# A long convolution and a spectral mix on one core: the places of the positions are permuted so that result weights and stores are neighbours

## The chip, the cores and the metric

The kernel runs on one core of one Trainium2 chip. The core has five engines with instruction streams of their own: TensorE (PE, matrix products; its weight loads are listed as PEld), VectorE (DVE), ScalarE (ACT), GpSimd (POOL) and SyncE (SP, which here only issues transfers). They meet at semaphores. Sixteen DMA engines move data between the chip's main memory (DRAM) and the on-chip SBUF; PE writes to PSUM, eight banks of 512 float32 columns on each of 128 partitions. The metric is the device time of one execution in microseconds (us).

## The reference: what is computed

Two layers, one behind the other. `x` is 8 sequences of 5696 positions with 128 channels, `h` a filter of the same length.

```python
# 1. causal long convolution along the sequence, by FFT of twice the length
Xf = np.fft.rfft(x, n=2*S, axis=1);  Hf = np.fft.rfft(h, n=2*S, axis=0)
v = np.fft.irfft(Xf * Hf[None], n=2*S, axis=1)[:, :S, :]
# 2. spectral mix: the lowest 64 modes are multiplied by complex 128x128 matrices
V = np.fft.rfft(v, axis=1);  Y = np.zeros_like(V)
Yr = einsum("bmd,mde->bme", Vr, w_r) - einsum("bmd,mde->bme", Vi, w_i)
Yi = einsum("bmd,mde->bme", Vr, w_i) + einsum("bmd,mde->bme", Vi, w_r)
Y[:, :64] = Yr + 1j * Yi
u = v + np.fft.irfft(Y, n=S, axis=1)
out = u + np.maximum(u @ w_ch, 0.0)          # (8, 5696, 128) float32
```

## The kernel before

The sequence's 5696 positions are written as 64 q + p, with q from 0 to 88 and p from 0 to 63. The transform is split into a step over q and one over p, both matrix products with constant tables. The 8 sequences go in 4 pairs. For each pair the kernel transforms, multiplies with the filter's transform (`products`) and transforms back over p, which gives Z: 180 rows (90 frequencies over q, real and imaginary) for each p and channel. Z is written to a scratch tensor in DRAM (`zscr`) and read again in the last stage. On the way the 64 lowest modes are summed up from Z (table G). This takes the first 264 us or so; then the modes are multiplied with `w_r`, `w_i` (`mix`), and the last stage begins.

**The last stage** (lines 777 to 932) runs over the four pairs `g_`. For a pair, Z is loaded in 4 chunks of 16 values of p (`load_zt`), into 5 chunk buffers, so 5 chunks ahead; the next load into a buffer is issued behind the u tiles that use it up. From it come two kinds of tile:

- A **u tile** (`u_tile`, `u_z`, `u_c`): 8 values of p, all 89 q, one sequence. 16 matmuls (8 values of p, real and imaginary rows) with Z as weights and 89 columns of table S4, and two with the mixed modes C as weights and 356 columns of table IB, add up in two PSUM banks. One instruction evacuates the 712 columns to float16 into UT, a buffer of 128 channels x 5696 positions, one for each sequence of the pair, with two sets of buffers in turn. It is done by ScalarE in five tiles of eight and by VectorE in three, in the last pair by ScalarE alone.
- A **result tile** (`o_tile`): up to 128 positions x 4. Four matmuls take 128 columns of UT as weights (line 889) and the 256 columns of WI (`w_ch` beside the identity), so that u and u @ w_ch of 128 positions stand in PSUM with the position on the partition. ScalarE takes the relu into R (line 896), VectorE adds u (line 897) into an output buffer, and SP stores it (line 908).

Both kinds take the next of four pairs of PSUM banks (`LSLOT`), so a tile can begin only when the tile four before it has left its banks.

How positions stand in UT: in the order of time, 64 q + p. A u tile of 8 values of p therefore writes groups of 8 float16 values, 64 apart. A result matmul's partition m takes position 44 m + 4 r4 + j, because then one partition's results are neighbours in DRAM: the weights are every 44th column of UT. Two such tiles (`wide`) fill one output buffer and one store of 512 KB, 4 KB a partition; 44 x 128 = 5632 positions leave 64 at the end (`TAIL`), which both sequences of a pair share in one tile of two matmuls. There are 7 wide output buffers and 4 small ones. As the weights span all of UT, a result tile needs all 8 u tiles of its sequence.

The order is written out by hand (lines 910 to 931). A list `todo` holds the result tiles that can be done. Behind each u tile one or two are taken from it (1 + half); in the last pair, where the sequences go one after the other, two, and two or three in the second sequence. A pair's result tiles are put in the list when the pair is done, those of the last pair's first sequence as soon as it is done. What is in the list after the last u tile is done then: the last pair's tail tile and the 11 tiles of the last sequence.

The symmetric tables S4 and IB are loaded for 33 of 64 values of p; `reflect` makes the others by reading backwards. All transfers named here are issued by SP, in the order of the program, so that a store that waits for its add holds up the loads behind it. Each store takes one of 12 semaphores in turn.

Of the kernel before, what the change touches and what calls it, by code (L numbers as in the profile page):

```python
# [4 lines left out]
P = 128  # L5
# [118 lines left out]
def bass_long_conv_fft__then__afno_spectral_mix_kernel(nc, x, h, moe_w_r, moe_w_i, moe_w_ch, out):  # L124
# [3 lines left out]
    J = 64  # L128
# [22 lines left out]
    c, s = np.cos(th), np.sin(th)  # L151
    w1 = np.block([[c, s], [-c, -s]])
    w2 = np.block([[-s, c], [-s, c]])
    back = np.full(NK, 2.0 * 4096.0 / L)
    back[0] = back[NK - 1] = 4096.0 / L
    pos = J * qq[None, :] + pp[:, None]
    ang = 2.0 * np.pi * kk[:, None, None] * pos[None] / L
    s4 = np.stack([back[:, None, None] * np.cos(ang), -back[:, None, None] * np.sin(ang)], axis=0)
    RB, PB = 2 * NK - P, 32
    rows = s4.transpose(1, 0, 2, 3).reshape(2 * NK, S)  # L160
    SH = (J // 2 + 1) * NQ
    s4t = np.zeros((P, 2 * SH))
    s4t[:, 0:SH] = rows[0:P, 0:SH]
    s4t[PB:PB + RB, SH:2 * SH] = rows[P:2 * NK, 0:SH]
# [127 lines left out]
    def pv(bank, off, dims, p0=0, n=P):  # L292
        return bass.AP(ps, p0 * 4096 + bank * 512 + off, [[4096, n]] + [list(d) for d in dims])
# [5 lines left out]
    def bank(i):  # L299
        return ("bank", i)  # L300
# [21 lines left out]
    def mm(o, l, r, st, sp, reads, writes):  # L322
        R.add("tensor", lambda h_: h_.matmul(o, l, r, start=st, stop=sp), reads, writes)  # L323
# [217 lines left out]

    def reflect(eng, t, n, col, key, after):
        MN = S - SH
        dst, src = bass.AP(t, SH, [[S, n], [1, MN]]), bass.AP(t, SH - NQ - 1, [[S, n], [-1, MN]])
        sc = sg_sb[0:n, col:col + 1]
        if eng == "scalar":
            R.add(eng, lambda e: e.activation(dst, src, COPY, scale=sc), [key + (0,), ("sg",)], [key + (1,)], after=after)
        else:
            R.add(eng, lambda e: e.tensor_scalar_mul(dst, src, sc), [key + (0,), ("sg",)], [key + (1,)], after=after)
# [225 lines left out]
        clear_zt(i)  # L775

    LSLOT = [0, 2, 4, 6]
    NCH = J // ZB
    n_ev = [0]
    ahead = {}  # L780
# [28 lines left out]
    def u_tile(i, b, half):  # L809
        g_, c_ = divmod(i, NCH)  # L810
        t = ahead.get((i, b, half))
        if t is None:
            t = u_z(i, b, half)
        else:
            for hb in range(2):
                u_c(i, b, half, t, hb, False)
        ub = (g_ % 2) * 2 + b
        old = {0: WT, 1: WT, 2: U_ALL, 3: U_ALL}[ub]
        n_ev[0] += 1
        e = "scalar" if n_ev[0] % 8 in (0, 2, 3, 5, 7) or g_ == NP - 1 else "vector"  # L820
# [42 lines left out]
    NW = S // P  # L863
    TAIL = S - NW * P

    def o_tile(g_, b, r4):
        ub = (g_ % 2) * 2 + b
        bb = 2 * g_ + b
        t = turns("l", LSLOT)
        i = n_o[0]  # L870
        n_o[0] += 1
        full = r4 < NW // 4
        ubs = [ub] if full else [ub, ub + 1]
        last_ = (g_, b) == (NP - 1, 1)
        wide = r4 < (8 if last_ else NW // 4 // 2 * 2)
        big = wide or (last_ and full)
        h_ = r4 % 2 if wide else 0
        if big:
            if not h_:
# [6 lines left out]
        n, rows = (4, P) if full else (2, TAIL)  # L886
# [4 lines left out]
        bk = [bank(t), bank(t + 1)] if full else [bank(t)]  # L891
        rs = r_sb[i % NR]
        rv = bass.AP(rs, 0, [[512, rows], [P, n], [1, P]])
        ov = bass.AP(ob, h_ * 512, [[OW, rows], [P, n], [1, P]])
        src_r, src_u = pv(t, 0, [[256, n], [1, P]], 0, rows), pv(t, P, [[256, n], [1, P]], 0, rows)
        R.add("scalar", lambda e: e.activation(rv, src_r, RELU), bk, [("r", i % NR)], after=once(("r", i % NR), G_ALL + XTT + [("y", 0), ("y", 1), ("id",)]))  # L896
        R.add("vector", lambda e: e.tensor_tensor(ov, src_u, rv, ADD), bk + [("r", i % NR)],  # L897
              [key + (h_,)], after=once(key, old))
        if wide and not h_:
            return  # L900
        w_ = (2 if wide else 1) * 4 * D
        if full:
            dst = bass.AP(out.tensor, out.offset + bb * S * D + (4 * r4 - 4 * h_) * D, [[NW * D, P], [1, w_]])
            src = ob[:, 0:w_]
        else:
            dst = bass.AP(out.tensor, out.offset + bb * S * D + NW * P * D, [[D, TAIL], [S * D, 2], [1, D]])
            src = bass.AP(ob, 0, [[OW, TAIL], [D, 2], [1, D]])
        dma("sync", dst, src, "o", [key + (v_,) for v_ in range(h_ + 1)])

    todo = []  # L910
    NB = NCH * NP
    NW4 = NW // 4
    for g_ in range(NP):
        last = g_ == NP - 1
        order = [(c_, b) for b in range(2) for c_ in range(NCH)] if last else [(c_, b) for c_ in range(NCH) for b in range(2)]
        for n, (c_, b) in enumerate(order):
# [47 lines left out]
```

## Time and profile before

| what | value |
|---|---|
| three runs of the kernel, us | 377.16, 378.18, 381.03 (median 378.18) |
| the profiled execution, us | 379.06 |
| its span, first to last instruction, us | 377.3 |
| granted TensorE clock | 0.995 |
| PE / PEld / DVE / ACT busy | 359.0 / 279.0 / 295.1 / 314.7 us |
| result matmuls (`ps<-WI,UT`) | 360, of which 8 in tail tiles |
| evacuations of u tiles | 46 on ACT at 752 ns, 18 on DVE at 890 ns |
| relu (line 896) and add (line 897) of a full result tile | 602 and 684 ns |
| stores to the output | 39 of 512 KB, 10 of 256 KB, 4 of 64 KB |
| first and last u tile evacuated, at | 265.5 us and 364.6 us |

How to read it: the profile is of one execution, and its times are from the start of the span; the time that a run is given is longer than the span by what lies around it, 1.8 us here. Busy times are sums over the whole span, over stages with different limits, so what counts for the change is read in the last stage alone. Matmuls are pipelined, so that one is busy for longer than the distance to the next. A group is one line of the kernel, one engine and one pair of tiles; line 323 is the helper that records every matmul, 311, 313, 315 and 317 are the helper that evacuates PSUM, 320 the one that issues transfers. A group's columns are: busy us, mean ns of one, idle us of the engine before them, and what ended that idle time.

### The profile page before, as it was taken

How to read it: one execution, taken by the hardware profiler on the slowest of the kernel's cores; microseconds unless marked ns; L12 is line 12 of the kernel's file. 1: busy time of each engine (PE TensorE's matmuls, PEld its weight loads, DVE VectorE, ACT ScalarE, POOL GpSimd, SP SyncE). 2: the span in 40 equal slices, each digit the busy share in tenths (PEclk: the TensorE clock that was granted, in tenths of full speed). 3: DMA queues.
4: the chain of work that ended last, by engine and by line, in shares of the span. 5: the costliest groups of instructions: out<-in, count | busy, mean ns of one | idle time of the engine just before them, and what ended most of it. 6: DMA issues, size and time to landing. Idle time of an engine off the chain costs nothing.

```text
span 377.3 us, 12488 instructions
## 1 busy us (share of the span) xinstructions
PE 359.0 (95%) x5370; PEld 279.0 (74%) x5370; DVE 295.1 (78%) x336; ACT 314.7 (83%) x495; POOL 75.4 (20%) x117
## 2 busy tenths in 40 slices
PE   7989989999999999999999999999999999999994
PEld 7878856666866666866667856667899989888873
DVE  3548889998898999998998988873547767756666
ACT  8468779998999997989997999996557677688885
POOL 8803011200552320743220401124000000000000
PEclk9998999999999999999999999999999999999999
DMA  7999959987899997899996899999999999999978
GB/s 145 209 289 363 242 148 200 264 214 225 130 159 197 221 265 221 95 144 207 256 261 178 85 292 344 336 364 351 366 408 394 414 418 407 414 404 384 362 303 343
DMA packets 87048, 103.94 MB, mean 276 GB/s; under 512 B 22730, under 2 KB 72522, under 8 KB 83438
## 3 DMA queue, kind: packets, MB, share of 16 engines
q1 hardware_dynamic: 64610, 81.33, 61.3%
q0 software_dynamic: 22384, 21.83, 35.0%
q8 instruction: 42, 0.69, 0.7%
q14 instruction: 12, 0.10, 0.1%
HBM read 70.61 MB, written 51.12 MB: 323 GB/s over the span
## 4 chain that ended last, share of the span: by engine, by line
PE 60%; ACT 15%; DMA 9%; DVE 7%; issue 4%; POOL 3%; SPq 1%; DVEq 0%; ACTq 0%; POOLq 0%
PE ps L323 60%; ACT As L313 7%; DMA out_dram<-O 4%; DMA Xr<-in_x_dram 4%; ACT Zs L311 2%; DVE As L317 2%; ACT Xs L311 2%; POOL Xr L320 2%; ACT Zt L311 2%; ACT R L896 1%; DMA Hs<-Hs 1%; DVE Xin L365 1%; POOL Hin L320 1%; DVE U L655 1%; DVE U L622 1%
## 5 line engine op out<-in xcount | busy, mean ns | idle before, releaser
L655 DVE TENSOR_TENSOR U<-Xs,Hs 128x2048 f16<-128x2048 f16 (+1 forms) x73 | 86.6, 1192 | 13.9 <-ACT Xs L311 12.9
L323 PE MATMUL ps<-U,Wc 128*128 128x512 f16 (+1 forms) x368 | 94.0, 376 | 1.4 <-DVE U L622 1.4
L311 ACT CAST Xs<-ps 128x1024 f16<-128x1024 f32 (+1 forms) x77 | 74.8, 978 | 9.9 <-PE ps L323 6.9
L311 ACT CAST Zs<-ps 128x512 f16<-128x512 f32 (+1 forms) x132 | 69.1, 594 | 1.7 <-PE ps L323 1.7
L897 DVE TENSOR_TENSOR O<-ps,R 128x512 f32<-128x512 f32 x81 | 52.3, 684 | 20.7 <-ACT R L896 11.3
L317 DVE TENSOR_SCALAR As<-ps 128x720 f16<-128x720 f32 (+1 forms) x67 | 55.8, 881 | 6.7 <-PE ps L323 5.2
L896 ACT ACTIVATE R<-ps 128x512 f32<-128x512 f32 (+1 forms) x92 | 50.5, 591 | 8.7 <-PE ps L323 8.6
L323 PE MATMUL ps<-F,Xin 128*128 128x180 f16 x512 | 53.5, 254 | 3.9 <-DVE Xin L365 2.4
L323 PEld LDWEIGHTS ps<-F,Xin 128*128 128x128 f16 x512 | 45.8, 155 | 11.2 <-DVE As L317 3.3
L323 PE MATMUL ps<-As,M 64*128 64x128 f16 (+2 forms) x1488 | 51.9, 215 | 1.3 <-ACT As L313 1.2
L313 ACT ACTIVATE As<-ps 128x720 f16<-128x720 f32 (+1 forms) x65 | 46.1, 768 | 8.2 <-PE ps L323 7.6
L323 PE MATMUL ps<-WI,UT 128*128 128x256 f16 x360 | 50.9, 278 | 0.5 <-ACT UT L311 0.4
L323 PEld LDWEIGHTS ps<-U,Wc 128*128 128x128 f16 x368 | 28.6, 97 | 30.3 <-ACT Zs L311 3.7
L311 ACT CAST UT<-ps 128x712 f16<-128x712 f32 x46 | 34.5, 752 | 18.2 <-PE ps L323 17.0
L323 PEld LDWEIGHTS ps<-As,M 64*128 64x128 f16 x1488 | 41.6, 94 | 7.6 <-ACT As L313 1.7
L323 PEld LDWEIGHTS ps<-WI,UT 128*128 128x128 f16 x360 | 39.0, 152 | 3.4 <-issue 1.8
L323 PE MATMUL ps<-IBs,C 128*128 128x356 f16 x128 | 39.2, 314 | 0.5 <-DVE O L897 0.4
L320 POOL DMA_DIRECT2D Xt<-in_x_dram x40 | 21.5, 542 | 80.5 <-PE ps L323 80.0
L323 PEld LDWEIGHTS ps<-G,Zs 128*128 128x128 f16 x512 | 26.1, 96 | 14.5 <-ACT Zs L311 2.0
L655 DVE TENSOR_TENSOR U<-ps,Hs 128x2048 f16<-128x2048 f32 x15 | 34.3, 2284 | 0.0
L323 PE MATMUL ps<-G,Zs 128*128 128x128 f16 (+2 forms) x512 | 32.2, 192 | 0.1
L311 ACT CAST Zt<-ps 128x512 f16<-128x512 f32 x52 | 28.5, 622 | 0.2 <-PE ps L323 0.2
(74 smaller groups left out, 483.1 us busy)
## 6 DMA issues: line engine op xcount, KB each, us to landing
out_dram<-O SPq DMA_DIRECT2D x39, 512.0 KB, 9.9
zscr<-Zs SPq DMA_DIRECT2D x62, 256.0 KB, 6.1
zscr<-Zt SPq DMA_DIRECT2D x26, 256.0 KB, 6.3
Xt<-in_x_dram POOLq DMA_DIRECT2D x20, 320.0 KB, 7.0
W<-wscr SPq DMA_DIRECT2D x4, 1024.0 KB, 7.7
ZT0a<-zscr SPq DMA_DIRECT2D x4, 1024.0 KB, 10.3
M<-cM POOLq DMA_DIRECT2D x5, 720.0 KB, 16.8
ZT1a<-zscr SPq DMA_DIRECT2D x3, 1024.0 KB, 11.0
```

Source lines behind the costliest of these rows:

```text
L311: R.add(e, lambda h_: h_.copy(dst, src), reads, writes, after=after)
L313: R.add(e, lambda h_: h_.activation(dst, src, COPY, scale=scale), reads, writes, after=after)
L317: R.add(e, lambda h_: h_.tensor_scalar_mul(dst, src, scale), reads, writes, after=after)
L320: R.add(eng, lambda h_: h_.dma_start(dst, src), reads, writes, ring=ring, after=after)
L323: R.add("tensor", lambda h_: h_.matmul(o, l, r, start=st, stop=sp), reads, writes)
L365: R.add("vector", lambda e: e.tensor_copy(bass.AP(x_sb, i * XN * XS, [[XW, NQ], [XS, XN], [1, D]]), src), list(toks) + XZ, [("xin", i)])
L622: R.add("vector", lambda e: e.tensor_tensor(bass.AP(u_s[0], b * 512 + d0, [[2048, P], [1024, 2], [D, n], [1, d1 - d0]]), bass.AP(s_[0], s_ ...
L655: R.add("vector", lambda e: e.tensor_tensor(uv, src, hv, MULT), bk + [("h", t, 0), ("h", t, 1, 0), ("h", t, 1, J)], [("u", i)])
L896: R.add("scalar", lambda e: e.activation(rv, src_r, RELU), bk, [("r", i % NR)], after=once(("r", i % NR), G_ALL + XTT + [("y", 0), ("y", 1 ...
L897: R.add("vector", lambda e: e.tensor_tensor(ov, src_u, rv, ADD), bk + [("r", i % NR)], [key + (h_,)], after=once(key, old))
```

## The change

The 64 values of p are renamed 8 A + j, with A and j from 0 to 7, and p = 8 A + j is put in place j * 8 + A, in every table (w1 and w2 by their columns, S4, IB and the modes by their rows). Position 64 q + 8 A + j is then 8 (8 q + A) + j.

- A u tile (8 places) now holds one j, all A, all q: 712 positions that are 8 apart in time. UT holds them as one run of 712 (`FR`), so that the evacuation writes neighbours.
- A result tile is one block `i` of 128 of these 712, for four values of j (half `h_`): its weights are 128 neighbouring columns of UT. Five blocks are full, the sixth has 72 rows. It needs only the four u tiles of its half.
- Two tiles (both halves of a full block) fill one store: partition m holds the 8 positions from 8 (128 i + m) on, so a store of 512 KB is one run in DRAM. The block of 72 rows is stored in two halves of 144 KB. In the last sequence all halves are stored by themselves (256 KB), each tile in a wide buffer of its own.
- A sequence has 12 result tiles, all of four matmuls; before, a pair had 22 of four and one of two.
- In the last pair, behind each u tile, two or three are taken from the list in the first sequence and three in the second. The last sequence's first half is put in the list when its first four u tiles are done; its second half, six tiles, is left after the last u tile.
- The mirror of a place is now 71 minus it, so 36 places of S4 and IB are loaded and 28 made by `reflect`.

```diff
+    order = np.arange(J).reshape(8, 8).T.reshape(J)
+    w1, w2 = [w[:, np.concatenate([order, J + order])] for w in (w1, w2)]
...
+    s4 = s4[:, :, order]
...
-    SH = (J // 2 + 1) * NQ
+    SH = (J // 2 + 4) * NQ
...
-    ib = ib.T.reshape(P, NQ, J).transpose(0, 2, 1)
-    mq = modes.reshape(NQ, J, P)
+    ib = ib.T.reshape(P, NQ, J).transpose(0, 2, 1)[:, order]
+    mq = modes.reshape(NQ, J, P)[:, order]
...
-        dst, src = bass.AP(t, SH, [[S, n], [1, MN]]), bass.AP(t, SH - NQ - 1, [[S, n], [-1, MN]])
+        dst, src = bass.AP(t, SH, [[S, n], [1, MN]]), bass.AP(t, SH - 1, [[S, n], [-1, MN]])
...
+    FR = S // 8
+    NF8 = (FR + P - 1) // P
...
-        evac(bass.AP(u_sb[ub], c_ * ZB + half * 8, [[S, P], [J, NQ], [4, 2], [1, 4]]),
+        evac(bass.AP(u_sb[ub], (2 * c_ + half) * FR, [[S, P], [8, NQ], [4, 2], [1, 4]]),
...
-    def o_tile(g_, b, r4):
+    def o_tile(g_, b, i, h_):
...
+        rows = min(P, FR - P * i)
+        big = rows == P
+        whole = big and bb < B - 1
+        hr = h_ if whole else 0
...
-        rd = [("u_", v_, c_) for v_ in ubs for c_ in range(2 * NCH)] + [("wch",), ("i16",)]
-        for j in range(n):
-            lh = bass.AP(u_sb[ub], 4 * r4 + j, [[S, P], [NW, P]]) if full else u_sb[ubs[j]][:, NW * P:S]
-            mm(pv(t + j // 2, (j % 2) * 256, [[1, 256]], 0, rows), lh, WI, True, True, rd, [bank(t + j // 2)])
+        rd = [("u_", ub, 4 * h_ + j) for j in range(4)] + [("wch",), ("i16",)]
+        for j in range(4):
+            mm(pv(t + j // 2, (j % 2) * 256, [[1, 256]], 0, rows),
+               bass.AP(u_sb[ub], (4 * h_ + j) * FR + P * i, [[S, P], [1, rows]]), WI, True, True, rd, [bank(t + j // 2)])
...
+        w_, c0 = (8, 0) if whole else (4, 4 * h_)
+        dma("sync", bass.AP(out.tensor, out.offset + (bb * S + 8 * P * i + c0) * D, [[8 * D, rows], [1, w_ * D]]),
+            ob[0:rows, 0:w_ * D], "o", [key + (v_,) for v_ in range(hr + 1)])
...
-                for _ in range((2, 2 + half)[n >= NCH] if last else 1 + half):
+                for _ in range((2 + half, 3)[n >= NCH] if last else 1 + half):
...
-                todo += [(g_, 0, r4) for r4 in range(NW4)]
-        todo += [(g_, 0, NW4)] * last
-        todo += [(g_, b, r4) for b in range(1 if last else 0, 2) for r4 in range(NW4)]
-        todo += [(g_, 0, NW4)] * (not last)
+                todo += [(g_, 0, r_, h_) for r_ in range(NF8) for h_ in range(2)]
+            if last and n in (NCH + NCH // 2 - 1, 2 * NCH - 1):
+                todo += [(g_, 1, r_, int(n == 2 * NCH - 1)) for r_ in range(NF8)]
+        if not last:
+            todo += [(g_, b, r_, h_) for b in range(2) for r_ in range(NF8) for h_ in range(2)]
```

More of the change, by code (lines that the diff above doesn't have):

```diff
@@ L862, in bass_long_conv_fft__then__afno_spectral_mix_kernel @@
     o_old = [H_ALL] * 2 + [M_ALL[5:6], U_ALL + [("f1",)]]
-    NW = S // P
-    TAIL = S - NW * P
-    def o_tile(g_, b, r4):
+    def o_tile(g_, b, i, h_):
         ub = (g_ % 2) * 2 + b
@@ L869, in o_tile @@
         t = turns("l", LSLOT)
-        i = n_o[0]
+        n_ = n_o[0]
         n_o[0] += 1
[L872 to L877, printed above, removed]
+        rows = min(P, FR - P * i)
+        big = rows == P
+        whole = big and bb < B - 1
+        hr = h_ if whole else 0
         if big:
-            if not h_:
+            if not hr:
                 o_cur[0] = turns("o8", list(range(NO8)))
@@ L885, in o_tile @@
         OW = 1024 if big else 512
-        n, rows = (4, P) if full else (2, TAIL)
-        rd = [("u_", v_, c_) for v_ in ubs for c_ in range(2 * NCH)] + [("wch",), ("i16",)]
-        for j in range(n):
-            lh = bass.AP(u_sb[ub], 4 * r4 + j, [[S, P], [NW, P]]) if full else u_sb[ubs[j]][:, NW * P:S]
-            mm(pv(t + j // 2, (j % 2) * 256, [[1, 256]], 0, rows), lh, WI, True, True, rd, [bank(t + j // 2)])
-        bk = [bank(t), bank(t + 1)] if full else [bank(t)]
-        rs = r_sb[i % NR]
@@ L893, in o_tile @@
[L893 to L898, printed above, removed]
@@ L899, in o_tile @@
-        if wide and not h_:
-            return
[L901 to L908, printed above, removed]
+        rd = [("u_", ub, 4 * h_ + j) for j in range(4)] + [("wch",), ("i16",)]
@@ new lines, in o_tile @@
+        for j in range(4):
+            mm(pv(t + j // 2, (j % 2) * 256, [[1, 256]], 0, rows),
+               bass.AP(u_sb[ub], (4 * h_ + j) * FR + P * i, [[S, P], [1, rows]]), WI, True, True, rd, [bank(t + j // 2)])
+        bk = [bank(t), bank(t + 1)]
+        rs = r_sb[n_ % NR]
+        rv = bass.AP(rs, 0, [[512, rows], [P, 4], [1, P]])
+        ov = bass.AP(ob, hr * 512, [[OW, rows], [P, 4], [1, P]])
+        src_r, src_u = pv(t, 0, [[256, 4], [1, P]], 0, rows), pv(t, P, [[256, 4], [1, P]], 0, rows)
@@ new lines, in o_tile @@
+        R.add("scalar", lambda e: e.activation(rv, src_r, RELU), bk, [("r", n_ % NR)], after=once(("r", n_ % NR), G_ALL + XTT + [("y", 0), ("y", 1), ("id",)]))
+        R.add("vector", lambda e: e.tensor_tensor(ov, src_u, rv, ADD), bk + [("r", n_ % NR)],
+              [key + (hr,)], after=once(key, old))
+        if whole and not h_:
+            return
+        w_, c0 = (8, 0) if whole else (4, 4 * h_)
+        dma("sync", bass.AP(out.tensor, out.offset + (bb * S + 8 * P * i + c0) * D, [[8 * D, rows], [1, w_ * D]]),
+            ob[0:rows, 0:w_ * D], "o", [key + (v_,) for v_ in range(hr + 1)])
@@ L910, in bass_long_conv_fft__then__afno_spectral_mix_kernel @@
     todo = []
     NB = NCH * NP
-    NW4 = NW // 4
     for g_ in range(NP):
         last = g_ == NP - 1
-        order = [(c_, b) for b in range(2) for c_ in range(NCH)] if last else [(c_, b) for c_ in range(NCH) for b in range(2)]
-        for n, (c_, b) in enumerate(order):
+        order_ = [(c_, b) for b in range(2) for c_ in range(NCH)] if last else [(c_, b) for c_ in range(NCH) for b in range(2)]
+        for n, (c_, b) in enumerate(order_):
             i = NCH * g_ + c_
```

## The prediction

> **What bounds the kernel now.** The change touches only the last stage, from about 264 us of the span to its end, and the constants loaded for it. I read the windows first, to see which engine is full there. Columns: window, length, then PE, PEld, DVE, ACT and POOL busy, granted clock, DMA share, GB/s.
>
> ```profile
> 300.00:310.00 10.00, 10.00 (x144) 8.82 (x143) 6.93 (x12) 7.39 (x13) 0.00 (x0) 1.00 1.02 419
> ...
> 340.00:350.00 10.00, 9.80 (x131) 8.54 (x128) 6.54 (x10) 8.56 (x16) 0.00 (x0) 1.00 0.95 382
> ...
> 360.00:370.00 10.00, 9.50 (x92) 7.69 (x92) 7.50 (x13) 9.06 (x17) 0.00 (x0) 1.00 0.77 305
> ```
>
> To 330 us PE is full and DMA is full too, at about 410 GB/s. Later DMA eases and ACT rises to 9 tenths. A pipelined PE shows itself busy in any case, so its pace is read from the timeline and its durations from the groups of 262 to 377 us.
>
> ```profile
> L323 PE MATMUL ps<-WI,UT 128*128 128x256 f16 x352 | 49.4, 278 | 0.2
> ...
> L323 PEld LDWEIGHTS ps<-WI,UT 128*128 128x128 f16 x352 | 38.4, 153 | 2.5 <-issue 1.7 <-ACT R L896 0.3
> ...
> L323 PEld LDWEIGHTS ps<-IBs,C 128*128 128x128 f16 x128 | 12.4, 97 | 4.0 <-ACT UT L311 1.7 <-issue 0.7 <-ACT C L313 0.2
> ```
>
> ```profile
> 301.16 0.87 PEld L323 LDWEIGHTS ps<-WI,UT 128*128 128x128 f16 x8
> 301.20 1.06 PE L323 MATMUL ps<-WI,UT 128*128 128x256 f16 x8
> ...
> 302.12 0.10 PEld L323 LDWEIGHTS ps<-IBs,C 128*128 128x128 f16 x1
> ...
> 303.08 0.44 PEld L323 LDWEIGHTS ps<-WI,UT 128*128 128x128 f16 x4
> 303.12 0.63 PE L323 MATMUL ps<-WI,UT 128*128 128x256 f16 x4
> ...
> 303.52 0.10 PEld L323 LDWEIGHTS ps<-IBs,C 128*128 128x128 f16 x1
> ```
>
> A u tile (18 matmuls) takes 303.08 - 302.12 = 0.96 us of PE, a result tile (4 matmuls) 303.52 - 303.08 = 0.44. The strided weights (every 44th column of UT) take 153 ns to load, the neighbouring ones 97. But eight result matmuls take 1.06 us, of which one is about 0.273 long: seven steps of 0.112. Single starts in the trace stand 0.109 apart except the first step of a run, 0.132. So the strided load is hidden behind the 256 columns that stream, but for about 0.023 us per run.
>
> In the last pair of sequences ScalarE evacuates every u tile, and its timeline gives the pace:
>
> ```profile
> 332.85 0.75 ACT L311 CAST UT<-ps 128x712 f16<-128x712 f32 x1 [0.40 <-PE ps L323]
> ...
> 344.70 0.75 ACT L311 CAST UT<-ps 128x712 f16<-128x712 f32 x1 [0.32 <-PE ps L323]
> ...
> 355.48 0.75 ACT L311 CAST UT<-ps 128x712 f16<-128x712 f32 x1 [0.70 <-PE ps L323]
> ...
> 364.60 0.75 ACT L311 CAST UT<-ps 128x712 f16<-128x712 f32 x1 [0.50 <-PE ps L323]
> ```
>
> 332.85 to 344.70 is six u tiles with two result tiles each: 1.975 us per u tile. 355.48 to 364.60 is four with 2.5 each: 2.28. Half a result tile more costs 0.305, a whole one 0.61, more than PE's 0.44: each waits for one of the four pairs of PSUM banks, which come free only after ScalarE's relu (602 ns) and VectorE's add (684 ns). After the last u tile VectorE sets the pace itself:
>
> ```profile
> 367.14 6.67 DVE L897 TENSOR_TENSOR O<-ps,R 128x512 f32<-128x512 f32 x11 [0.18 <-issue]
> ```
>
> Eleven adds in 6.67: (6.67 - 0.68)/10 = 0.60 a tile. Last the chain that ended last, which shows one other limit:
>
> ```profile
> 328.96 15.85 DMA out_dram<-O
> ...
> 344.93 0.70 DVE O L897
> ```
>
> A store issued at 328.96 landed 15.85 us later, and an add waited for its buffer (0.3 us in the waits). Landing took 9.5 us for the first store, at 283; in the two middle pairs DMA is asked for more than it carries, and the seven wide output buffers just cover that.
>
> **Part by part.**
>
> *Result tiles.* Before, a pair had 22 full tiles and one of two matmuls: 90 matmuls. Now a sequence has 712 rows of 8 positions, that is five blocks of 128 and one of 72, times two halves: 24 full-priced tiles and 96 matmuls a pair, since a tile of 72 rows streams the same 256 columns. In the second and third pair's stages the six matmuls are PE work: 2 x 6 x 0.109 = **+1.3 us**. In the last stage, 23 + 23 tiles become 24 + 24: 44 full ones and two half ones (about 0.38, from the relu's 378 ns and the add's 411) become 48: 4 x 0.60 - 2 x 0.38 = **+1.6**.
>
> *The last sequence in halves.* After the last u tile six tiles remain, not twelve; before it stand 42 for 34, six moved there and two new. A tile costs 0.60 to 0.61 there and 0.60 in the tail. Moving is worth **0**. Its bounds: three tiles per u tile, all along, are not in the trace; at PE's 0.44 the eight would gain 8 x 0.16 = 1.3, at 0.62 they lose 0.2. I take the measured 0.61.
>
> *Neighbouring weights.* 16 runs of result matmuls in each of two PE-bound stages, 0.023 us each: **-0.7** (0 if the banks take it up again, -1.1 if the last stage gains too). The Trainium skill, "SBUF — State Buffer", section "Door 1: The DMA port swizzle", says that an access which crosses to a new 16-byte line pays a penalty. The trace agrees in the load's own time, 153 against 97 ns; the pace of 0.109 says that it is hidden.
>
> *UT written without gaps.* ScalarE took 594 ns for 512 columns and 978 for 1024 in other groups, whose output has no such gaps; that line gives 744 for 712, and UT takes 752. At most 46 x 8 ns = 0.4 beside waits: **0**. VectorE's 18 at 890 ns stand likewise near the 881 of a 720-column eviction.
>
> *Stores.* The bytes are the same. 512 KB stores land neighbouring, no longer 22.5 KB apart; a 4 KB packet takes 159 ns, and 8 KB read 309, the same rate, so I see no gain to be had in the order: **0**. There are 61 stores for 53; SP spends 0.33 us on each and waits 55.8 us for VectorE, so 8 more are hidden, but what waits in SP's order behind a store is the next load of Z, ahead by more than 10 us. A store's semaphore is used again after 12 stores: about 19 us at the new pace of the last stage, 15.9 is the longest landing. The wide buffers do matter: the last stage takes 2.5 tiles per u tile from its start on, 0.91 us a tile for 0.99. The buffer of its first store is wanted again after some 15 tiles, 13.7 us, while stores then take about 15 to land: a stall of 1.3 for the 0.3 of now, **+1.0**. Below: 0, if the middle stages, now longer, let DMA catch up; above +2.6, when landing grows to 16 us.
>
> *Constants.* Three tables grow from 33 to 36 places: 68 + 68 + 45 KB, 0.43 us at 410 GB/s, in a stretch where DMA is full; PE waited 0.2 for a piece of Z at about 271 us. I take **+0.2** (0 to 0.45). The reflected parts shrink by a tenth: 931 ns becomes some 840, on VectorE beside PE: 0. The permuted weights have the same shapes: 0.
>
> *The end.* The last store is 144 KB for 256: landings there were 3.0 us for 256 KB, 2.5 for 64: **-0.3**.
>
> Sum: 1.3 + 1.6 + 0 - 0.7 + 1.0 + 0.2 - 0.3 = **+3.1 us**. The profiled execution took 379.06 with a span of 377.3; it becomes 382.2 with 380.4. The median of the runs is 0.9 below the profiled one: 378.2 + 3.1 = **381.3**.
>
> **Rivals.**
>
> *Stores become the bound (slower).* From a landing of about 14 us on, each us more at the start of the last stage is a stall, and repeats as the seven buffers come round, until the backlog is gone. For it: 15.85 already reached. Against it: the demand per us falls a little. What could add to it are the 16 stores of 72 rows: 72 packets of 2 KB at 84 ns are 0.4 us over 16 engines and 6 over a single one, and the trace does not show how they spread. At two stalls of some 2 to 3 us and the rest of the sum: about 384.5. The Trainium skill, "DMA: Bandwidth & Descriptors", section "Why a DMA increments its semaphore by 16 and not by 1", says that a transfer issued by SP runs on the largest number of engines up to 16 that divides its outer size: 12 for 72 rows. By that these stores take 6 x 84 = 0.50 us for 0.38, an estimate of +0.1 each; no row here shows it.
>
> *Moved tiles are cheap (no change).* If result tiles between u tiles cost nearer PE's 0.44 once banks are taken in another order, 1.3 goes, and with it the stall may be small: 378 to 379.5.
>
> *Weights were on the path (faster).* If 56 ns were won for each of 352 loads: -19.7 us and the rest of the sum without its 0.7: about 362. The 0.109 pace, equal to the other groups' per streamed column (0.078 for 180), speaks against it.
>
> *The change does not do what it says*: the loads stay at 153 ns, because the time is not the stride's. Then 0.7 comes back: 382.
>
> **How the numbers follow.** Chances: forecast 0.50 (380 to 382.8), stores 0.20, cheap tiles 0.18, unchanged loads 0.08, weights 0.04. One per cent, about what a measurement of this kernel can tell from no change, is 3.8 us: 374.4 to 382.0. Faster: 0.04 and 0.01 from the cheap tiles. Slower: 0.20, 0.04 of the unchanged loads, and 0.15 of the forecast: 0.39. The rest, 0.56, within. The low ends of the terms sum to about 0, the high ones to +6; the range 377.8 to 385.0 leaves out the weights, the cheap tiles' lower end and the stores' upper one.
>
> **What would show it.** Loads of WI,UT at about 97 ns and result matmuls still 0.109 apart, 384 of them; the second and third stage 0.3 us longer each; evacuations of UT 2.28 apart in the first half of the last stage and about 2.6 in the second; six adds after the last u tile for twelve, 0.60 apart; a wait of an add for a store of about 1 us near 345. The prediction is wrong if result tiles in the last stage cost other than 0.60, or if landings exceed 17 us or stay below 13.

## Result and the profile after

The changed kernel takes 382.6 us (median of six runs, 381.77 to 384.26), the kernel before 378.6 beside it (377.16 to 381.03): a ratio of 1.0108 [1.0082, 1.0134], 4.0 us more. The profiled execution takes 382.0 with a span of 380.2, for 379.06 and 377.3 before: 2.9 more. Forecast were +3.1 and 381.3. The total was met; its terms were not all, and the table shows which. It cuts both profiled spans at the same marks: the starts of the evacuations of u tiles 18, 34 and 50 (the second of each later pair) and of u tile 64, the last; then the end of the last add, and the end of the span.

| stretch, us | before | after | difference | forecast |
|---|---|---|---|---|
| up to u tile 18 | 281.17 | 281.17 | 0.00 | +0.2 constants |
| 18 to 34, second pair | 26.47 | 26.87 | +0.40 | +0.3 |
| 34 to 50, third pair | 27.09 | 27.92 | +0.83 | +0.3 |
| 50 to 64, last pair | 29.87 | 34.14 | +4.27 | |
| 64 to the last add | 9.20 | 5.82 | -3.38 | |
| the last two together | 39.07 | 39.96 | +0.89 | +1.6 tiles, +1.0 stall |
| last add to the end | 3.47 | 4.28 | +0.81 | -0.3 |

The windows, with the columns as in the prediction (window, length, PE, PEld, DVE, ACT, POOL busy, granted clock, DMA share, GB/s), say that the bounds stayed where they were, and that the last stage asks more of DMA near its end: a share of 0.83 for 0.77.

```profile
300.00:310.00 10.00, 10.00 (x145) 8.34 (x144) 7.25 (x12) 7.55 (x13) 0.00 (x0) 1.00 1.03 411
...
340.00:350.00 10.00, 10.00 (x131) 8.04 (x130) 6.81 (x12) 8.03 (x15) 0.00 (x0) 1.00 0.91 368
...
360.00:370.00 10.00, 10.00 (x124) 7.94 (x121) 7.56 (x14) 9.05 (x16) 0.00 (x0) 1.00 0.83 313
```

The groups of the result matmuls after (262 to 381 us, shapes apart; busy us and mean ns, then idle before and its releaser). In the changed kernel the helper lines are 326 for matmuls, 314, 316, 318 and 320 for evacuations, and 323 for transfers.

```profile
L326 PE MATMUL ps<-WI,UT 128*128 128x256 f16 x320 | 43.6, 272 | 0.6 <-ACT UT L314 0.4 <-DVE O L897 0.2
L326 PEld LDWEIGHTS ps<-WI,UT 128*128 128x128 f16 x320 | 27.8, 97 | 6.5 <-issue 1.5 <-ACT UT L314 1.4 <-ACT R L896 0.5
L326 PE MATMUL ps<-WI,UT 128*72 128x256 f16 x64 | 8.9, 272 | 0.0
...
L326 PEld LDWEIGHTS ps<-WI,UT 128*72 128x72 f16 x64 | 6.1, 112 | 1.1 <-ACT UT L314 0.5 <-ACT R L896 0.3 <-issue 0.2
```

320 and 64 make the 384 foretold. A full load takes 97 ns where it took 153, and a matmul for 72 rows lasts the same 272 ns as one for 128: small tiles are indeed full-priced on PE. The timeline of one u tile and its result tiles:

```profile
301.08 0.80 PEld L326 LDWEIGHTS ps<-WI,UT 128*128 128x128 f16 x8
301.12 1.04 PE L326 MATMUL ps<-WI,UT 128*128 128x256 f16 x8
...
303.01 0.36 PEld L326 LDWEIGHTS ps<-WI,UT 128*128 128x128 f16 x4
303.05 0.60 PE L326 MATMUL ps<-WI,UT 128*128 128x256 f16 x4
...
303.45 0.10 PEld L326 LDWEIGHTS ps<-IBs,C 128*128 128x128 f16 x1
```

Eight matmuls in 1.04 us, before 1.06: the load is a third shorter and the run gains 0.02, its first step. Four take 0.60 for 0.63.

The pace of the last pair, from ScalarE's timeline:

```profile
341.04 0.75 ACT L314 CAST UT<-ps 128x712 f16<-128x712 f32 x1 [0.93 <-PE ps L326]
...
350.15 0.75 ACT L314 CAST UT<-ps 128x712 f16<-128x712 f32 x1 [0.52 <-PE ps L326]
...
355.15 0.75 ACT L314 CAST UT<-ps 128x712 f16<-128x712 f32 x1 [0.39 <-PE ps L326]
...
370.11 0.75 ACT L314 CAST UT<-ps 128x712 f16<-128x712 f32 x1 [0.39 <-PE ps L326]
```

341.04 to 350.15 is four u tiles with 2.5 result tiles each: 2.28, as forecast. 355.15 to 370.11 is six with three each: 2.49, where 2.6 was forecast. Half a tile more costs 0.21 there, that is 0.42 a tile. This is close to PE's bare 0.44, and not the 0.61 of the step from two to 2.5.

The tail, from VectorE's timeline:

```profile
371.44 0.69 DVE L897 TENSOR_TENSOR Os<-ps,R 72x512 f32<-72x512 f32 x1 [0.79 <-issue]
372.25 3.08 DVE L897 TENSOR_TENSOR O<-ps,R 128x512 f32<-128x512 f32 x5
375.25 0.68 DVE L897 TENSOR_TENSOR Os<-ps,R 72x512 f32<-72x512 f32 x1
```

The first row is still the last tile of the first half. The six adds of the last half follow, 0.60 apart ((375.25 - 372.25)/5). The stall that the forecast put at 1.0 us stands in the chain and, with 0.4 us, in the waits (longest first, total, count, longest):

```profile
323.64 15.26 DMA out_dram<-O
...
339.02 0.70 DVE O L897
```

```profile
DVE O L897 <- DMA out_dram<-O: 0.4, 1, 0.4
```

Last the stores, by the time that SP takes for one issue (ns, shortest/median/longest, first and last start):

```profile
L323 SPq DMA_DIRECT2D out_dram<-O x45: 332/429/1708, 283.2 to 375.9; - x45
L323 SPq DMA_DIRECT2D out_dram<-Os x16: 325/796/1770, 293.2 to 376.4; - x16
```

The same line of before:

```profile
L320 SPq DMA_DIRECT2D out_dram<-O x42: 332/333/578, 283.2 to 373.8; - x42
```

An issue took 0.33 us in the median before. After, it took 0.43 for a wide store and 0.80 for one of 72 rows, and up to 1.77; in all SP spent 39.4 us on 61 stores, 20.3 on 53 before. The last store was issued 0.46 us after the last add, before 0.03. And the transfers were further behind. From the semaphore events of each store, the wide one issued at about 360 us landed after 6.4 us, before after 3.5; the stores issued from 371 us on landed after 3.4 to 4.0 us, those of before from 367.5 on after 2.5 to 3.0. The last store's later issue (0.4) and its later landing (3.4 us for 3.0) are the +0.8 of the end.

What the runs had to tell apart: whether the loss is the added result work, with its stores of 72 rows, and the neighbouring weights give little back; or whether the new order of the last pair is at fault (the list in halves, tiles moved in between), or the use of the wide buffers (the stall), or the end.

### The profile page after: what moved, and what is told of

It reads as the page before. It is cut to its first block, busy times and chain, and to the rows that moved or that the text cites. A ratio compares the mean times of both kernels' runs of the same rounds, so it can differ in the third digit from the quotient of the medians.

```text
span 380.2 us, 12559 instructions
## 1 busy us (share of the span) xinstructions
PE 359.0 (94%) x5394; PEld 272.9 (72%) x5394; DVE 298.2 (78%) x340; ACT 316.5 (83%) x499; POOL 75.2 (20%) x117
## 4 chain that ended last, share of the span: by engine, by line
PE 66%; ACT 10%; DMA 10%; DVE 6%; issue 3%; POOL 3%; DVEq 0%; POOLq 0%
PE ps L326 66%; ACT As L316 7%; DMA out_dram<-O 4%; DMA Xr<-in_x_dram 4%; DMA Xt<-in_x_dram 2%; DVE As L320 2%; POOL Xr L323 2%; DVE U L625 1%; ACT Zs L314 1%; ACT Xs L314 1%; POOL Hin L323 1%; DVE Xin L368 1%; DVE Hs L318 1%; DVE O L897 1%; ACT R L896 1%
## 5 line engine op out<-in xcount | busy, mean ns | idle before, releaser
L896 ACT ACTIVATE R<-ps 128x512 f32<-128x512 f32 (+1 forms) x96 | 52.9, 600 | 8.3 <-PE ps L326 8.3
L326 PE MATMUL ps<-F,Xin 128*128 128x180 f16 x512 | 52.4, 249 | 4.5 <-DVE Xin L368 3.1
L326 PEld LDWEIGHTS ps<-F,Xin 128*128 128x128 f16 x512 | 44.4, 155 | 11.9 <-DVE As L320 3.2
L326 PE MATMUL ps<-WI,UT 128*128 128x256 f16 (+1 forms) x384 | 52.2, 272 | 0.6 <-ACT UT L314 0.4
L326 PEld LDWEIGHTS ps<-WI,UT 128*128 128x128 f16 (+1 forms) x384 | 33.9, 100 | 7.6 <-ACT UT L314 1.9
```

## Experiments

All but two are the changed kernel with one edit; e9 and e12 are the kernel before with one. Ratios are to the kernel before on the same chip, with the 95% interval.

### The changed kernel again: e5

No edit. It stands beside e6, e7 and e8.

> The changed kernel itself once more, so that the other runs stand beside it on one chip: 382 to 383, 1.0 to 1.1 per cent over before.

381.57 us, 1.0086 [1.0049, 1.0124]. Its profiled stretches: 26.87, 27.92, 33.61, 5.95, 4.56; no add waited for a store. So the two pairs' stages repeat to 0.01 us, the last pair varies by 0.4 (39.56 for 39.96), which is the 0.43 of the wait, and the end by 0.3. What follows is read against both profiles.

### The same amount of result work: e4

```diff
+        n = 2 if (i, h_, b) == (NF8 - 1, 1, 0) else 4
...
+            ... for r_ in range(NF8) for h_ in range(2) if (b, r_, h_) != (1, NF8 - 1, 1)
```

For each pair, one tile of 72 rows is left out and another has two matmuls, with the relu, add and store to match: 90 result matmuls, 22 whole tiles and a half one, as before the change. The places, order and halves are those of after. The stores are fewer than before the change, too: what is left out is not stored, 216 KB a pair, so 21,920 KB go out for 22,784, in 57 stores, 12 of them of 72 rows.

> The changed kernel with as much result work as before: of the blocks of 72 rows, the second sequence of each pair leaves out the second half, and the first one does two of four matmuls in its second half, with relu and add of half the columns and a store of half the bytes. So 90 result matmuls a pair and 22 full tiles and one half. Theory (the added tiles are the loss): 378.5 to 379.5, as before the change. Rival (the layout, the order or the stores lose it): 381.5 or more.

377.66 us, 0.9973 [0.9949, 0.9997]: a little faster than the kernel before. Its stretches are 26.21, 27.08, 33.42, 5.23, 3.01. Beside e5:

| what the left out work costs | us | forecast |
|---|---|---|
| second and third pair | 0.66 + 0.84 | 0.65 + 0.65 |
| last pair to the last add | 0.91 (1.31 with after's profile) | 1.6 |
| the end | 1.55 | 0 |

Together 3.96, as much as the whole loss, for the added work and its stores together. In the second pair's stage it is the work: the distances between result matmuls sum up to 8.64 us in e5 and 7.99 in e4, 0.65 for six matmuls, and all other steps of PE are the same within 0.01. Beside the kernel before, e4 is 0.26 and 0.01 shorter in the two pairs, 0.42 in the last pair and 0.46 at the end. The first two are the weights (see e9); the other two cannot be put down to the layout, the order or the halves, since e4 also stores 864 KB less. An issue of its wide stores is back at the 0.333 us of before, in the median:

```profile
L323 SPq DMA_DIRECT2D out_dram<-O x45: 332/333/942, 282.5 to 372.4; - x45
```

### Neighbouring weights alone: e9

```diff
-            lh = bass.AP(u_sb[ub], 4 * r4 + j, [[S, P], [NW, P]]) if full else ...
+            lh = bass.AP(u_sb[ub], (4 * r4 + j) * P, [[S, P], [1, P]]) if full else ...
```

The kernel before, with 128 neighbouring columns of UT as weights for every 44th. Its output rows are then other positions than those that they are stored as.

> The kernel before the change, where only the result matmuls' weights are taken as 128 neighbouring columns of UT for every 44th; the results are then stored at wrong positions, all else stays. Theory (hidden but for 0.023 us in the first step of each run): loads from 153 to 97 ns, full steps 0.109 as before, 0.3 less in the stages of the second and third pair, 0.7 less in all, 377.7 for the 378.4 of before. Rival (worth nothing): 378.4. Rival (weights on the path): 362 to 370.

378.45 us, 1.0013 [0.9992, 1.0034]. The groups (262 us to the end):

```profile
L323 PE MATMUL ps<-WI,UT 128*128 128x256 f16 x352 | 48.1, 272 | 0.2
...
L323 PEld LDWEIGHTS ps<-WI,UT 128*128 128x128 f16 x352 | 30.5, 97 | 6.8 <-issue 3.2 <-ACT R L896 0.5
```

The loads fall from 153 to 97 ns, 7.9 us of busy time in all, and the runs' time does not move. The two stages are 0.12 and 0.16 us shorter, 0.28 for the forecast 0.7. The mean distance of result matmuls fell from 115 to 110 ns, 0.78 us in the two stages, but the steps from a result tile to the u tile behind it grew by 0.51: from 281 to 335 us PE's loads wait 1.1 us for evacuations of u tiles, which free the banks, and 0.2 before. e4's 0.26 + 0.01 is the same amount. The 56 ns of each load were hidden.

### A short stride: e6

```diff
-    bass.AP(u_sb[ub], (4 * h_ + j) * FR + P * i, [[S, P], [1, rows]])
+    bass.AP(u_sb[ub], (4 * h_ + j) * FR + (i if big else P * i), [[S, P], [FR // P if big else 1, rows]])
```

The weights of a full block are every fifth column (10 bytes), and its store's rows lie five times as far apart.

> The changed kernel, u still written as a run of 712, but a full block takes every 5th of 640 columns, so that the result weights are strided (10 bytes) and a store's 4 KB pieces are 20 KB apart in DRAM, nearly as before the change. Theory (strided loads are hidden but for 0.023 us in the first step of a run, and the order of the stores in DRAM is worth nothing): loads of about 150 ns, full steps 0.109, the stages of the second and third pair 0.3 longer each; 0.7 to 1.1 over the changed kernel beside it. Rival (neighbouring weights or stores carry more): over it by 2 or more. Rival (worth nothing): the same.

382.41 us, 1.0116 [1.0078, 1.0154].

```profile
L326 PEld LDWEIGHTS ps<-WI,UT 128*128 128x128 f16 x320 | 31.6, 118 | 3.6 <-issue 1.3 <-ACT UT L314 1.3 <-ACT R L896 0.5
```

118 ns, where I had expected about 150: the load's time goes with the stride, 97 neighbouring, 118 at 10 bytes, 153 at 88. The second pair's stage is 26.87 in e6, e5 and after: neither the load nor the pitch of the stores shows in it. The third is 1.4 longer, with one gap of 1.57 us on PE at 323.5 that no other engine ends (see e8; 0.48 in e5). The intervals of e6 and e5 overlap.

### Strided weights with the changed order: e1

```diff
-        evac(bass.AP(u_sb[ub], (2 * c_ + half) * FR, [[S, P], [8, NQ], [4, 2], [1, 4]]),
+        evac(bass.AP(u_sb[ub], 2 * c_ + half, [[S, P], [J, NQ], [32, 2], [8, 4]]),
...
-               bass.AP(u_sb[ub], (4 * h_ + j) * FR + P * i, [[S, P], [1, rows]]), ...
+               bass.AP(u_sb[ub], 4 * h_ + j + 8 * P * i, [[S, P], [8, rows]]), ...
```

UT in the order of time again, so that u tiles write and result tiles read every eighth column.

> The changed kernel, but u is written in the order of time again (groups of 8 apart), so that the result weights are every 8th column of UT; tiles, order and stores stay. Theory (the strided load is hidden behind the 256 streaming columns but for the first step of a run): loads go from 97 back to about 150 ns, full steps stay 0.109, the first step of a run goes from 0.109 to 0.132; 48 runs at 0.023 are 0.7 to 1.1 us, so 383.3 to 383.7 for the 382.6 of the changed kernel. Rival (the neighbouring weights carry a real share, masked by the added tiles): +3 us or more, 385.6 and up. Rival (they are worth nothing): 382.6.

491.36 us, 1.2965 [1.293, 1.300], and not through the weights. The groups of the evacuations in e1:

```profile
L314 ACT CAST UT<-ps 128x712 f16<-128x712 f32 x46 | 152.7, 3421 | 16.2 <-PE ps L326 16.2
...
L318 DVE CAST UT<-ps 128x712 f16<-128x712 f32 x18 | 59.5, 3354 | 9.5 <-PE ps L326 9.5
```

The same ones after the change:

```profile
L314 ACT CAST UT<-ps 128x712 f16<-128x712 f32 x46 | 34.5, 752 | 18.1 <-PE ps L326 17.6
...
L318 DVE CAST UT<-ps 128x712 f16<-128x712 f32 x18 | 16.1, 892 | 8.8 <-PE ps L326 8.8
```

Writing each float16 16 bytes behind the last makes ScalarE take 3421 ns where it took 752, and VectorE 3354 where it took 892; the 64 evacuations then bound the stage. In its window ScalarE is busy for all of the 20 us and the granted clock is down to 0.74:

```profile
280.00:300.00 20.00, 14.71 (x160) 11.75 (x160) 10.52 (x4) 20.00 (x9) 0.00 (x0) 0.74 0.49 180
```

So the run does not answer its question. It answers another: the kernel before wrote groups of eight float16, 16 bytes, and paid nothing for the gaps (752 both times). The Trainium skill, "SBUF — State Buffer", section "Door 1: The DMA port swizzle", names a penalty for each crossing to a new 16-byte line. The trace agrees in kind: eight times as many lines for the same 712 values take 4.5 times as long (3421 to 752).

### The last sequence whole: e2

```diff
-                for _ in range((2 + half, 3)[n >= NCH] if last else 1 + half):
+                for _ in range((2, 2 + half)[n >= NCH] if last else 1 + half):
...
-            if last and n in (NCH + NCH // 2 - 1, 2 * NCH - 1):
-                todo += [(g_, 1, r_, int(n == 2 * NCH - 1)) for r_ in range(NF8)]
+            if last and n == 2 * NCH - 1:
+                todo += [(g_, 1, r_, h_) for r_ in range(NF8) for h_ in range(2)]
```

The tiles per u tile of the kernel before, and all of the last sequence's tiles in the tail.

> The changed kernel without the halves of the last sequence's release: its 12 result tiles come behind the last u tile, and in the last pair two, and then two or three, are taken as before the change. Theory (a result tile costs about 0.60 between u tiles and 0.60 behind them): the same as the changed kernel, 382.6 within 0.6. Rival (between u tiles it costs only what PE takes, 0.44, so that releasing six of them early wins 6 x 0.16): 1.0 slower, 383.6.

381.36 us, 1.0074 [1.0045, 1.0104], within the interval of e5. 50 to 64 takes 29.45 and the tail 10.41, together 39.86; e5 has 39.56, after 39.96. Moving six tiles out of the tail is worth 0, give or take 0.4. The rival of the new order falls. The evacuations of the last pair are 1.98 us apart with two tiles per u tile and 2.27 with 2.5, as in the kernel before (1.98 and 2.28): the new layout does not change the price of that step.

### The wide buffers: e11 and e7

e11 has six wide output buffers for seven:

```diff
-            [a_xt + 4096 * i for i in range(2)]
+            [a_xt + 4096 * i for i in range(1)]
```

> The changed kernel with six wide output buffers for seven. Theory of the forecast (seven just cover the landings at the start of the last stage): an add waits for a store by 2 us or more there, 384 or more. Rival (there is slack, the forecast's stall was not there): within 0.5 of the changed kernel, 381.6 to 382.6.

383.42 us, 1.0146 [1.0117, 1.0175]. Its waits:

```profile
DVE O L897 <- DMA out_dram<-O: 2.0, 1, 2.0
```

e7 puts the 72-row tile of the last sequence's halves first, so that the last store has 128 rows:

```diff
-                todo += [(g_, 1, r_, ...) for r_ in range(NF8)]
+                todo += [(g_, 1, r_, ...) for r_ in [NF8 - 1] + list(range(NF8 - 1))]
```

> The changed kernel, but among the six last result tiles the block of 72 rows comes first and not last. Theory (the last store lands late because it is one of 72 rows): from the last add to the end 3.3 us for 4.3, so 1.0 less than the changed kernel beside it. Rival (a backlog of all stores on part of the DMA engines makes the end late, whichever is last): within 0.4 of it, the end still 4 or more.

381.26 us, 1.0081 [1.005, 1.0111], as e5. Its waits:

```profile
DVE O L897 <- DMA out_dram<-O: 1.8, 2, 1.3
```

The wait of an add for a store is real and grows with one buffer less (the last pair takes 42.74 us in e11, 3.2 more than in e5), but with seven it is 0.0 in e5, 0.4 in after, 1.8 in e7: seven buffers stand at the edge, and small shifts decide. Little of e7's wait stays in the times: its last pair is 1.3 us longer than e5's and its end 0.6 shorter, and the medians of e5 and e7 differ by 0.3. The end takes 4.00 us in e7, 2.64 in e11, where the last store has 72 rows and DMA had 3 us more to catch up. So the kind of the last store does not set the end; the backlog does.

### Fewer rows stored: e3

```diff
+        srows = rows if big else 64
...
-            ob[0:rows, 0:w_ * D], ...
+            ob[0:srows, 0:w_ * D], ...
```

Of each block of 72 rows only 64 are stored; 262 KB in all are left out.

> The changed kernel, but the stores of the blocks of 72 rows store only 64 of them; 8 rows of each such half, 64 KB a sequence in all, are left out of the output. Theory (72 rows are taken by fewer DMA engines than 64 or 128 and hold up SP's issues and the last landing): SP's issues in the last pair fall from 0.5 to 1.8 us back to 0.33, the time from the last add to the end goes from 4.3 to about 3.5, 381.6 to 381.9. Rival (the row count doesn't matter, the long issues come from the number of stores): 382.4 to 382.6, issues as long as now.

379.79 us, 1.0031 [1.0008, 1.0054]. The end takes 2.73. Stores issued at 360 us land after 2.6 us (after: 6.4), and SP's issues are short again in the median, 0.338 us for a wide store and 0.477 for a 64-row one (after: 0.429 and 0.796 for a 72-row one):

```profile
L323 SPq DMA_DIRECT2D out_dram<-O x45: 332/338/1391, 281.6 to 374.1; - x45
L323 SPq DMA_DIRECT2D out_dram<-Os x16: 472/477/1592, 291.6 to 374.7; - x16
```

262 KB are 0.6 us at 410 GB/s; 1.8 us against e5 and 2.8 against after are more, and the run is shorter than either expectation. In the profiles the end is 1.83 shorter than e5's and the last pair 0.12; the second pair's stage is 26.87 as in e5, so the bytes do not show there. (The third is 0.84 longer, with a gap on PE of the kind told at e8.) The semaphore events say what differs: a store of 128 or 64 rows makes 16, one of 72 makes 13, one soon after its issue and 12 more; loads of Z with 52 rows make one and 13, stores of eight rows (in e10) one and eight. That is the rule of the Trainium skill, "DMA: Bandwidth & Descriptors", section "Why a DMA increments its semaphore by 16 and not by 1", of which the prediction said that no row showed it: 72 rows go through 12 engines. That these 12 then run late is argued. Of the 16 events of the wide store issued at 355.10 us in after, four came by 2.8 us and twelve from 3.2 to 7.7, which fits it; of the one at 360.43, nine came by 3.9 us and seven up to 6.4, which fits it less.

### All rows, in 64 and 8: e10

```diff
+        for r0, r1 in ((0, P),) if big else ((0, 64), (64, rows)):
+            dma("sync", ... [[8 * D, r1 - r0], [1, w_ * D]]), ob[r0:r1, 0:w_ * D], ...)
```

> The changed kernel, but each store of 72 rows is issued as one of 64 and one of 8 rows, so all output is stored and the 64 rows can spread evenly; 16 issues of SP more. Theory (72 rows load 12 of the DMA engines more, and that costs 1 to 2 us): 379.8 to 380.8, last add to the end 3 us or less. Rival (the kernel with 64 rows won by the bytes that it left out): 381.5 to 382.5.

381.48 us, 1.0095 [1.007, 1.012]: no gain. Most of the backlog is gone (landings of 2.2 to 4.0 us near 360), but SP now spends 42.2 us on issuing 77 stores, and the last goes out about 1.0 us after the last add:

```profile
L323 SPq DMA_DIRECT2D out_dram<-Os x32: 472/496/1561, 292.3 to 376.4; - x32
```

Two gaps of 0.85 and 0.75 us on PE that no engine ends (306.1 and 324.2) lie in the middle pairs. So e3's gain is that of the 72-row stores, but how much of it is their bytes and how much their 12 engines is open, since e10 pays for its 16 further issues and its gaps may have given DMA time.

### Rows spread more evenly: e8

```diff
-        rows = min(P, FR - P * i)
-        big = rows == P
+        rows, f0 = BLOCKS[i]
+        big = i < NF8 - 1
...
+    BLOCKS = [(P, P * k) for k in range(4)] + [(120, 512), (80, 632)]
```

> The changed kernel with the 712 rows of a sequence cut into 4 blocks of 128, one of 120 and one of 80, for 5 of 128 and one of 72; all output is stored, with as many tiles and matmuls. Theory (a store of 72 rows loads part of the DMA engines more, and that is what the kernel with 64 rows stored won): 379.5 to 380.5, some 2 to 3 less than the changed kernel beside it, and a wait of an add for a store no longer there. Rival (the 64 rows won by the bytes left out, or by chance): 382 or more.

388.03 us, 1.0244 [1.0204, 1.0284], 6.5 more than e5. 80 rows go through 16 engines, 120 through 15 (by the events). The chain and the windows:

```profile
300.00 15.61 PE ps L326 x222
315.61 4.25 issue
319.86 25.19 PE ps L326 x316
```

```profile
310.00:320.00 10.00, 5.75 (x82) 4.75 (x81) 5.61 (x9) 4.26 (x8) 0.00 (x0) 0.91 1.00 368
320.00:330.00 10.00, 10.00 (x113) 8.67 (x111) 4.26 (x7) 5.93 (x10) 0.00 (x0) 0.75 0.89 356
```

PE stands still for 4.25 us while nothing in the trace holds it ("issue"). In that time one 16 KB packet of an instruction queue moves, at 317.48; DMA is at 1.00. Afterwards the granted clock is 0.75 for a window. A like gap stands near 324 in other kernels: 0.48 us from one matmul's start to the next in after, e2, e5 and e7, 1.0 in e3, 1.6 in e6, in after, e3 and e6 some 0.8 to 1.7 us behind such a packet; before has none of this kind above 0.33. That PE waits for its instructions behind a full DMA is argued from this nearness; no run separates it.

The gap does not explain all of e8. Its last pair takes 39.46 us as in e5, but its end 5.60; stores issued at 360 us land after 8.3 us, and SP's issues take 0.51 us (wide) and 0.93 (80 rows) in the median. So stores that use 15 or 16 engines had a backlog too, which speaks against the 12 engines as the whole cause of it. But e8's packets are slower as well (from 340 us on, 4 KB in 179 ns for after's 165), and why is open, so that e8 settles nothing about the rows.

### More result tiles without stores, in the kernel before: e12

```diff
+        todo += [(g_, 0, NW4), (g_, 0, NW4 - 1, False), (g_, 0, NW4, False)] * (not last)
...
-        if wide and not h_:
+        if not store or wide and not h_:
```

The work that the change adds, one full tile and half a tile a pair, without a store.

> The kernel before the change with as much result work as the changed one: a pair does one full tile and one of two matmuls once more (matmuls, relu and add), without a store. Theory (the added tiles are most of the loss): 0.65 a stage in the second and third, 0.60 a tile in the last pair, +2.6 to +2.9, 381.0 to 381.3. Rival (most of it is in the stores of 72 rows): +1.5 or less, below 380.

384.6 us, 1.0171 [1.0151, 1.0191], more than the change itself, for a reason of its own. The waits:

```profile
PE ps L323 <- DVE UT L315: 1.4, 1, 1.4
...
PE ps L323 <- ACT UT L311: 0.8, 1, 0.8
```

One tile slipped behind the u tile that writes its UT buffer anew and waits for it, with PE gaps of 1.6 and 1.0 us. The reason is the list: one or two tiles are taken from it per u tile, 24 a pair, and a pair now puts in 25. So of the 24 added matmuls only two fall into each of the two pairs' stages and 20 into the last pair. The two stages are 1.9 and 1.5 longer, without the whole gaps 0.3 and 0.5, which says nothing on the 0.65 of six matmuls. The last pair is 2.8 longer for five tiles more, whole and half, that come in the tail: 0.56 a tile. As a measure of stores against matmuls the run failed.

## Why the prediction came out as it did

- **Result tiles in the pairs' stages, +1.3.** Right: six matmuls take 0.65 us in the second pair's stage (e5 against e4), as forecast. In the third pair's 0.84 lie the 0.45 of the gap near 324, which e4 does not have there; e4 loses some 0.3 in a gap of its own.
- **Result tiles in the last stage, +1.6.** The count was right, the price too high: 0.9 (e5 against e4), or 1.3 with after, where 0.4 of waiting for a store is in it. (e4 also stores less; e3, with 256 KB less to store, is 0.12 shorter there.) The step that failed is "A tile costs 0.60 to 0.61 there": that held for the step from two to 2.5 tiles per u tile (before and e2), not from 2.5 to three, where it is 0.42. By the prediction's own sign, result tiles that cost other than 0.60, its account of the last stage was wrong, though the total was met. Why the further half tile is cheaper stays open. Here the rival of the moved tiles had the price right, but not the sum that it drew from it.
- **Moving tiles out of the tail, 0.** Shown by e2, to 0.4 us.
- **Neighbouring weights, -0.7.** Mis-sized, nearer to the 0 that was its upper bound: 0.28 by e9, 0.27 by e4, and not measurable in e9's time. The mechanism (hidden load, first step alone) held, and so did the size on PE (0.78 in e9); the waits for banks took 0.5 of it. The rival of unchanged loads fell with 97 ns, that of weights on the path with e9.
- **UT without gaps, 0.** Held: 752 ns before and after. What the forecast had not seen is how near a cliff lies (e1).
- **The stall, +1.0.** Mis-sized: with seven buffers 0.4 after and 0.0 in e5, though 1.8 in e7. The longest landing was 15.63 us, not above the 15.85 of before. That the middle pairs, longer by 1.2, let DMA catch up is the reason that the lower bound named; no run separates it.
- **Constants, +0.2.** 0.00 between the two profiles, and no PE wait for Z near 271 came of it. But this says little: the profiles of the changed kernel and of its variants (e2 to e8, e10, e11), which are the same up to there but for the first result tiles, reach u tile 18 at between 279.56 and 281.17 us. The term cannot be told from nothing.
- **Store order 0, eight more issues hidden.** The place and pitch of stores showed no cost (e6). The hiding of the issues failed at the end: "8 more are hidden" went by 0.33 us an issue, and an issue grew to 0.43 in the median and 1.77 at most.
- **The end, -0.3.** The sign was wrong: +0.8 in the profile, +1.1 in e5. The step took the last store's own size for what sets the end; what sets it is the backlog of DMA, as e7 excludes the last store's kind and e11, with the same stores and 3 us more time, ends in 2.64. That the 72-row stores make the backlog is shown by e3 (2.73) as far as their bytes and their engines go together; which of the two it is stays open (e8, e10). The prediction set aside the 12 engines of a 72-row store as a rival's, at an estimated +0.1 us each; 16 such stores make 1.6, and e3, which has none, has an end 1.8 shorter than e5's. That the two are near each other proves nothing, as e8's stores of 80 rows do no better.

So that the total of 3.1 was met (2.9 in the profile, 4.0 in the runs) was luck: errors cancelled. Against after's profile, 1.7 was too much for the last pair's tiles and stall and 0.2 for the constants; 0.6 was too little in the two pairs' stages (0.4 for the weights, 0.2 for the rest) and 1.1 too little at the end. The rival "stores become the bound" was right that transfers fall behind, with the 72-row stores in it; but it looked for the loss in stalls at the start of the last stage, and what the stores cost came at the end.

## What to carry to other kernels

Making a weight load a third shorter gains next to nothing when it is hidden behind its matmul's columns: read the distance between matmul starts, not the load's duration. When a layout leaves a remainder, count what the remainder costs in full-priced tiles and in stores of their own, before anything that the layout tidies: here 96 matmuls for 90 a pair and 16 stores of 72 rows outweighed all gains (e4, with less of both, takes 4 us less than e5). When tiles are added between others, measure their price at that number of tiles: the step from two to 2.5 did not hold for the step to three. What ends last is not always the last thing issued: see how long the transfers of the last 20 us take to land.

## What the runs showed of the hardware that was not expected

- Writes of single float16 values 16 bytes apart take 3421 ns on ScalarE and 3354 on VectorE for 128 x 712, against 752 and 892 for neighbouring values (e1, after); groups of eight with gaps between take 752 on ScalarE (before).
- A load of 128 float16 weight columns takes 97 ns neighbouring, 118 at 10 bytes, 153 at 88 bytes and 157 at 16 bytes (e1).
- SP's issue of a store is no constant: for a wide one 0.33 us in the median before and in e4, 0.43 after, and up to 1.77 for one of 72 rows, where landings lag.
- The events of one store come unevenly: of the 16 of a wide store (after, issued at 360.43 us) four had come by 3.8 us and the last came at 6.4; before, at 359.88, the 16 lie between 2.4 and 3.5.
- PE can stand for 0.5 us (after, e5) to 4.25 us (e8) with nothing in the trace that holds it, near a 16 KB packet of an instruction queue, with DMA at a share of 1.00 in e8. Whether the packet is the cause is not shown.
